# Another order for the pieces between the steps of the first down projection, and a later request for one weight block

## The chip, the core and the metric

The kernel runs on one core of a Trainium2 chip. The time is device microseconds (us) of one execution, smaller is better. The core's engines each work through an instruction queue of their own, in order: TensorE (PE; the profile counts its weight loads apart, as PEld), VectorE (DVE), ScalarE (ACT), GpSimd (POOL) and SyncE (SP). Here SP and POOL mostly issue DMA transfers. Engines wait for each other by semaphores.

## The reference

A transformer block over 2048 tokens of width 576, in bfloat16: a modulated layer norm, local attention with 32 heads of 18 (each token sees itself and seven earlier ones, two apart), an output projection, and a gated feed-forward of width 4608, with six modulation rows computed from a condition vector. Cut to what matters:

```python
mod = (_silu(c) @ w_mod).reshape(1, 6, 1, -1)            # sa, ca, ga, sb, cb, gb
h = _layernorm(x) * (1 + ca) + sa
q, k, v = split_heads(h @ wqkv)                          # 32 heads of 18
logits = einsum('bhsd,bhswd->bhsw', q, k[:, :, s - 2 * w]) * 18 ** -0.5   # w = 0..7, masked where s < 2w
o = einsum('bhsw,bhswd->bhsd', softmax(logits), v[:, :, s - 2 * w])
x = x + ga * (o @ wo)
h = _layernorm(x) * (1 + cb) + sb
x = x + gb * (((h @ w_gate) * (h @ w_up)) @ w_down)
```

## The kernel before, in words

**Tokens.** The 2048 tokens are 16 tiles of 128. Attention goes by chunks of 256 tokens (two tiles; chunks 0 to 7). The feed-forward goes by five groups of tiles, `GROUPS = [(0, 2), (2, 6), (6, 10), (10, 13), (13, 16)]`: chunk 0 alone, then chunks 1 and 2, then 3 and 4, and so on. The width 576 is four rows of 128 and one of 64; 4608 is 36 tiles f in nine weight blocks of four.

**Stages.** For each group, `gate_up` (from L847) goes through the 36 f: 18 matmuls, each on one half of PE's rows, fill two PSUM banks (`pg`, `pu`); ACT copies them out (L874, L875) and DVE multiplies them into `hh` (L880). After every fourth f, `ahead` (L892) asks for the next block of gate and up weights, on SP's queue. Then `down_pairs` (from L906) multiplies `hh` with the down weights, whose blocks POOL's queue loads (L173). For the first group, the down stage is 32 steps of 0.49 us, four to a block, each of four 512-wide and four 64-wide half matmuls (`acc` and `accr`, all issued in the helper `half`, L558), and then the last block in four runs. Four of the eight PSUM banks hold these sums; the other four make two pairs, which the pieces below take in turn. A third piece waits until the first one's pair has been read out.

**Pieces.** All work of later chunks is cut into pieces that are put between the steps. After step n, the pieces of the list at n are issued, in order; `dbg[0]` (L1466) is the plan of the first down stage, a list of (n, pieces) in which a pair of pieces takes n and n + 1. Since every engine's queue runs in order, the place in this plan is also the place in each engine's queue. The pieces, with i the chunk:

- `o_parts(i)` (L670): PE turns the attention output `o_sb` into `oT` (first and second half of the transposes); ACT copies it out (L640 ff.).
- `w1`, `w2` (`w_units`, L646): the output projection from `oT` and `wo`, in two column halves of two parts each; DVE scales it by `ga` (L656) and adds the residual `x_r` (L658): `x1`.
- `a_parts(i)` (L673): PE turns the normed input `xn` into `hT`; `mod_evict` (L630) scales and shifts it on the way out, half of it on DVE (three L327) and half on ACT (three L329).
- `q3, k3, qk4_3, v0_3, v1_3` (`qkv_units`, L685): chunk 3's query, key and value projections from `hT`.
- `av(n)` (`B_av`): the next n of chunk 2's weighted value sums on DVE (L543, L550, L552), which end in `o_sb` (L554, L555).
- `stat1`, `stat4`: statistics of chunk 1's `x1` and of chunk 4's input on ACT (L311, L314); `norms(n1)`, `norms(n4)` norm them on DVE (L322). `norm_x1_2` (L1449) does both for chunk 2's `x1`: one tile's statistics on ACT, the other's on DVE (L1456, L1457), then the norms (L322, L1462).
- `b_parts(i)` (L679): as `a_parts`, from the normed `x1` to `h2T`, which the next `gate_up` reads; `t2_2` is `b_parts(2)`. Normed tiles `ln_xn` have two buffers.

`a_parts(4)` and the projections of chunks 4 and 5 lie in the second `gate_up`, the latter between the f that `units` (L1478) names.

**Loads.** `gb_row` (L1367) runs right before the first step. It issues, on POOL and SP, down blocks 1 to 4, chunk 2's value rows (`b_ld(2, 0)`, `b_ld(2, 1)`: `vsh`, 1152 KB each) and the second group's gate/up blocks 10 and 11, and `behind` makes the latter wait until down block 3 has landed. Block 9, the first that the second `gate_up` uses, has been asked for in `ahead(0, 6)`, in the last third of the first `gate_up`. Down blocks 5, 6, 8 and 7 follow (in this order) as steps free their buffers; block 7 is used from step 28.

Of the kernel before, what the change touches and what calls it, by code (L numbers as in the profile page):

```python
# [21 lines left out]
KT = 5  # L22
# [6 lines left out]
FT = FF // P  # L29
# [6 lines left out]
FB = 4  # L36
# [12 lines left out]
def kernel(  # L49
# [97 lines left out]
    NBLK = FT // FB  # L147
# [224 lines left out]
    aa, bb, h2T, x1 = {}, {}, {}, {}  # L372
# [257 lines left out]
    def mod_evict(dst, cols, vi, kf=KF, on_dve=True):  # L630
        n = P * len(cols)

        def out_(a, b):
            for m in range(KF):
                modulate(dst(m), (a, b)[m // 2][:, m % 2, 0:n], m, vi + 1, vi, on_dve and m < 2)
            for h, t in enumerate((a, b)):
                modulate(half_of(dst(KF), h), t[:, 2, 0:n // 2].rearrange("p (c t) -> p c t", t=64), kf, vi + 1, vi, on_dve and h == 0)
        return out_
# [31 lines left out]
    def o_parts(i):  # L670
        return parts(lambda: turn_unit(o_sbs[i % 2], (0, 1), o_evict))

    def a_parts(i):  # L673
        def make():
            a_tiles(i)
            return turn_unit(aa[i]["xn"], (0, 1), mod_evict(lambda m: aa[i]["hT"][:, m, :], (0, 1), 0, KT))
        return parts(make)

    def b_parts(i, cols=(0, 1)):  # L679
# [212 lines left out]
    def ahead(gi, n):  # L892
        g = gi * NBLK + n + 2
        if gi > 0:
            load_wgu(g)
        elif n in (1, 2, 3):
            load_wgu(g + 2)
        elif n == 4:
            load_wgu(NBLK - 1)
        elif n == 5:  # L900
            load_pair_rows()
            load_wo_rows()
        elif n == 6:
            load_wgu(NBLK)

    def down_pairs(gi, hh, bg):  # L906
        for piece in bg.get(-1, ()):
            piece()
        t0, t1 = GROUPS[gi]
        nj = t1 - t0  # L910
        steps = down_steps(nj)
        acc = [ps([P, 512], F32, "acc") for _ in range(2)]
        accr = [ps([P, 2, 64], F32, "accr") for _ in range(3 if nj == 3 else 2)]
        acc += [ps([P, 512], F32, "acc") for _ in range(nj - 2)]
        o_ts, t_r = {}, {}
        seen, written, order, synced = set(), {}, [0], [-1]
        left = {("a", j): 2 * FT for j in range(nj)} | {("r", j): 2 * FT for j in range(nj)}

        def mm(kind, j, r, f):
            bank = (kind, j) if kind == "a" else (kind, j % len(accr))  # L920
            dst = acc[j][:] if kind == "a" else accr[j % len(accr)][:, j // len(accr), :]
            cs = slice(0, 512) if kind == "a" else slice(512, D)
            last_r, n, m = written.get(bank, (r, -1, None))
            if last_r != r and n > synced[0]:
                swap_after(m)
                synced[0] = n
            rows = (LO, HI)[r]
            left[kind, j] -= 1
            m = half(dst, hh[rows, f, js(j)], wd_blk[gi * NBLK + f // FB][rows, f % FB, cs], bank not in seen, left[kind, j] == 0)
            seen.add(bank)  # L930
            written[bank] = (r, order[0], m)
            order[0] += 1

        def pair(kind, lo, hi):
            for r, (j, f) in enumerate((lo, hi)):
                mm(kind, j, r, f)

        def gate(j):
            o_ts[j] = gup.tile([P, 512], BF, name="o_t", tag="g_sb" if j % 2 else "u_sb")
            nc.vector.tensor_tensor(o_ts[j][:], acc[j][:], gb_bc[:, 0:512], ALU.mult)  # L940

        def gate_r():
            t = smp.tile([P, nj, 64], BF, name="t_r", tag="tree")
            for k, a in enumerate(accr):
                n = len(range(k, nj, len(accr)))
                nc.vector.tensor_tensor(t[:, k:nj:len(accr), :], a[:, 0:n, :],
                                        gb_bc[:, None, 512:D].to_broadcast([P, n, 64]), ALU.mult)
            t_r[0] = t

        for n, (lo, hi, r_early, loaded) in enumerate(steps):  # L950
            fs = list(zip(lo, hi))
            for k, (a, b) in enumerate(fs):
                if r_early and k == len(fs) - 1:
                    pair("r", a, b)
                    pair("a", a, b)
                else:
                    pair("a", a, b)
                    pair("r", a, b)
            if loaded is not None and (gi > 0 or loaded not in (4, 5)):
                load_wd((5, 6, NBLK - 1, 7)[loaded] if gi == 0 and loaded < 4 else gi * NBLK + loaded + 3)  # L960
            for piece in bg.get(n, ()):
                piece()
        f0 = FT - FB

        def run(kind, a, b):
            for f in range(f0, FT):
                pair(kind, (a, f), (b, f))

        if nj == 2:
            run("r", 0, 1)  # L970
            run("a", 0, 1)
            for piece in bg.get(len(steps), ()):
                piece()
            run("r", 1, 0)
            gate_r()
            run("a", 1, 0)
            gate(0)
            gate(1)
        elif nj == 4:
            run("r", 0, 1)  # L980
            run("r", 2, 3)
            run("a", 0, 1)
            run("a", 2, 3)
            run("r", 1, 0)
            run("r", 3, 2)
            gate_r()
            run("a", 1, 0)
            gate(0)
            gate(1)
            run("a", 3, 2)  # L990
            gate(2)
            gate(3)
        else:
            for k, (lo, hi) in enumerate(cycle_of_three(f0)):
                for a, b in zip(lo, hi):
                    pair("a", a, b)
                    pair("r", a, b)
                if k == 4:
                    gate(1)
            gate_r()  # L1000
            gate(0)
            gate(2)
        assert not any(left.values())
        for j in range(nj):
            xt = x1[(t0 + j) // ST][(t0 + j) % ST]
            r0 = (t0 + j) * P
            nc.vector.tensor_tensor(xt[:, 0:512], o_ts[j][:], xt[:, 0:512], ALU.add)
            nc.vector.tensor_tensor(xt[:, 512:D], t_r[0][:, j, :], xt[:, 512:D], ALU.add)
            nc.sync.dma_start(out_flat[r0:r0 + P, :], xt[:])
        load_wd(gi * NBLK + NBLK + 2)  # L1010
# [362 lines left out]
    def gb_row():  # L1373
        p_t = mod_row(lambda k: wm5[:, k, :] if k < KF else wm5r[:], sc32)
        rows = gup.tile([P, RN], BF, name="gb_rows", tag="u_sb")
        nc.scalar.copy(rows[0:32 * RG, :], p_t[0:32 * RG, :])
        nc.sync.dma_start(gd[:], rows[0:32 * RG, :])
        nc.sync.dma_start(gb_bc[:], bass.AP(gd.tensor, gd.offset, [[0, P], [32 * RN, RG], [1, RN]]))
        behind(load_wd(1), wgu_in[7])
        load_wd(2)  # L1380
        b_ld(2, 0)
        place_pair_rows()
        wd3 = load_wd(3)
        for g in (1, 2):
            behind(load_wgu(NBLK + g), wd3)
        b_ld(2, 1)
        load_wd(4)


    def av(n):  # L1390
        for p in av2[:n]:
            p()
        del av2[:n]
# [20 lines left out]
    w1, w2, w3, w4, w5, w6, w7 = [w_parts(i) for i in range(1, NCH)]  # L1414
# [17 lines left out]
    def norms(n):  # L1432
        for j in range(ST):
            n["norm"](j)
# [14 lines left out]
    def norm_x1_2():  # L1449
# [11 lines left out]
        for d0, s0, n in ((0, 0, D), (D, D - 64, 64)):  # L1461
# [2 lines left out]
    q3, k3, qk4_3, v0_3, v1_3 = qkv_units(3, [(0, 0, 5)])[0]  # L1464
    t2_2 = b_parts(2)
    dbg = {0: at((-1, [gb_row]), (-1, lambda: n3["rsq"]()), (0, o_parts(1)), (0, lambda: (norms(n3), load_x(5))), (2, lambda: av(4)),  # L1466
                 (5, a_parts(3)), (6, stat4), (6, lambda: av(2)), (7, w1[0]), (9, w1[1]), (10, stat1), (11, q3), (12, lambda: av(3)), (13, k3), (14, lambda: av(14)),
                 (15, qk4_3), (17, v0_3), (19, lambda: norms(n1)), (20, o_parts(2)), (22, lambda: (norms(n4), load_x(6))), (22, b_parts(1)), (24, w2[0]),
                 (25, w2[1]), (26, norm_x1_2), (28, v1_3), (FT - FB - 1, t2_2)),
           1: at((0, o_parts(3)), (3, w3[0]), (6, w3[1]), (8, lambda: b_ln(3)), (9, o_parts(4)), (10, lambda: b_norm(3)), (13, b_parts(3)),  # L1470
                 (13, lambda: a_ln(6)), (16, w4[0]), (18, lambda: (a_norm(6), load_x(8))), (19, w4[1]), (21, lambda: b_ln(4)),
                 (23, a_parts(6)), (24, lambda: b_norm(4)), (28, b_parts(4))),
# [2 lines left out]
                 (24, a_parts(7)), (25, lambda: b_norm(6)), (29, b_parts(6, (0,)))),  # L1475
           3: at(*apart(3, b_parts(6, (1,))), *apart(9, o_parts(7)), *apart(16, w7[0]), *apart(23, w7[1]), (27, lambda: b_ln(7)),
                 (33, lambda: b_norm(7)), *apart(41, b_parts(7)))}
    units = {1: qkv_units(4, [(2, 0, 1), (3, 1, 2), (4, 2, 3), (5, 3, 4), (6, 4, 5)]) | qkv_units(5, [(29, 0, 1), (30, 1, 2), (31, 2, 3), (32, 3, 4), (33, 4, 5)]),  # L1478
             2: qkv_units(6, [(0, 0, 1), (1, 1, 2), (2, 2, 3), (3, 3, 4), (4, 4, 5)]),
             3: qkv_units(7, [(0, 0, 3), (1, 3, 4), (2, 4, 5)])}  # L1480
    for gi in range(NG):
# [37 lines left out]
```

## Time and profile before

| | |
|---|---|
| runs | 546.92, 545.93, 546.80 us; median 546.8 |
| the profiled execution | 546.86 us, of which the span is 545.2 |
| PE busy | 535.3 us, 98% of the span |
| DVE, ACT, POOL busy | 319.8, 268.5, 72.0 us |
| granted TensorE clock | 1.000 |
| first gate/up ends, down stage begins | 88 us |
| second gate/up begins | 121 us |
| DMA in this stretch (88 to 116 us) | 305 to 336 GB/s |

The span is the time from the first to the last instruction that the profile shows. A line of the waits names the engine and the line that waited, what released it, the time in all, how often and the longest. A row of the timeline gives start, duration, engine, line, operation, output and inputs, and in brackets the engine's idle time before it with the releaser; "issue" means that the profile shows nothing that it waited for. A matmul's duration is longer than its step to the next, since matmuls overlap.

### The profile page before, as it was taken

The page shows a single profiled execution, that of the slowest core. Times are in us where ns is not written, and L with a number is a line of the kernel's source. Part 1 is how long each engine was busy: PE and PEld are TensorE (multiplying, and loading weights), DVE is VectorE, ACT ScalarE, POOL GpSimd, SP SyncE. Part 2 cuts the span into 40 slices and gives each one's busy share as a digit, 9 for nine tenths or more (in the row PEclk, how much of TensorE's full clock was granted, in tenths as well). Part 3 has the DMA queues.
Part 4 walks back from the last instruction along what each step waited for, and adds up shares of the span by engine and source line. Part 5 has one row for each costly group of instructions (what it writes and reads, how often), then busy time and mean ns, then how long its engine had stood idle before and what let it go on. Part 6 is the DMA issues. An engine that isn't in the chain of part 4 may idle for free.

```text
span 545.2 us, 17482 instructions
## 1 busy us (share of the span) xinstructions
PE 535.3 (98%) x7579; PEld 339.6 (62%) x7579; DVE 319.8 (59%) x775; ACT 268.5 (49%) x657; POOL 72.0 (13%) x117
## 2 busy tenths in 40 slices
PE   7999999999999999999999999999999999999997
PEld 4788887656544698755544445556665555666564
DVE  7887898966469862557357795454537624322203
ACT  2766687755655763213656653224566511556500
POOL 4301224130001001112000101111100023100010
PEclk9999999999999999999999999999999999999999
DMA  8999999968336844346533774444785766965021
GB/s 261 279 266 316 352 303 340 338 196 293 96 115 217 275 136 143 112 117 231 210 108 127 259 235 156 133 132 133 237 269 155 231 198 176 348 193 175 1 88 34
DMA packets 70775, 108.83 MB, mean 200 GB/s; under 512 B 4234, under 2 KB 58458, under 8 KB 70698
## 3 DMA queue, kind: packets, MB, share of 16 engines
q1 hardware_dynamic: 59440, 61.76, 37.2%
q0 software_dynamic: 11168, 45.81, 25.5%
q8 instruction: 59, 0.97, 0.8%
q14 instruction: 18, 0.15, 0.1%
q10 hardware_dynamic: 90, 0.15, 0.1%
HBM read 103.22 MB, written 4.48 MB: 198 GB/s over the span
## 4 chain that ended last, share of the span: by engine, by line
PE 85%; DMA 8%; DVE 3%; ACT 2%; issue 1%; SPq 0%; POOL 0%; POOLq 0%; ACTq 0%; DVEq 0%
PE pg L558 26%; PE pu L558 21%; PE acc L558 17%; PE pp L558 9%; PE acc L1050 4%; DMA vsh<-vd 3%; DMA wgu<-in_B_w_up_dram 2%; PE accr L558 2%; DMA wv<-in_A_wqkv_dram 1%; PE lg L486 1%; DMA wmA<-in_w_mod_dram 1%; DVE prod L476 1%; PE pq L415 1%; PE po L759 1%; PE tr_pA L605 1%
## 5 line engine op out<-in xcount | busy, mean ns | idle before, releaser
L558 PE MATMUL pg<-h2T,wgu 64*128 64x512 bf16 (+2 forms) x1440 | 280.4, 333 | 1.0 <-issue 1.0
L558 PE MATMUL pu<-h2T,wgu 64*128 64x512 bf16 (+2 forms) x1440 | 278.7, 333 | 0.0
L558 PEld LDWEIGHTS <-wgu 64*128 64x128 bf16 x2880 | 148.4, 94 | 97.7 <-issue 1.3
L874 ACT CAST u_sb<-pu 128x512 bf16<-128x512 f32 (+2 forms) x180 | 90.1, 501 | 126.2 <-PE pg L558 118.2
L880 DVE TENSOR_TENSOR hh<-g_sb,u_sb 128x512 bf16<-128x512 bf16 (+2 forms) x180 | 66.3, 370 | 104.8 <-ACT g_sb L875 102.6
L558 PE MATMUL acc<-wd,hh 64*128 64x512 bf16 x888 | 118.3, 377 | 0.0
L558 PEld LDWEIGHTS <-hh 64*128 64x128 bf16 x1872 | 66.9, 94 | 43.9 <-issue 0.2
L875 ACT CAST g_sb<-pg 128x512 bf16<-128x512 f32 (+2 forms) x180 | 91.5, 508 | 0.0
L558 PE MATMUL accr<-wd,hh 64*128 64x64 bf16 x888 | 80.2, 189 | 0.0
L558 PE MATMUL pg<-h2T,wgr 64*128 64x512 bf16 (+2 forms) x180 | 60.1, 334 | 0.5 <-ACT h2T L329 0.5
L558 PE MATMUL pu<-h2T,wgr 64*128 64x512 bf16 (+2 forms) x180 | 60.1, 334 | 0.0
L173 POOL DMA_DIRECT2D wd<-in_B_w_down_dram x38 | 28.7, 755 | 176.6 <-PE accr L558 74.3
L476 DVE TENSOR_TENSOR prod<-qT,kT 128x1280 bf16<-128x1280 bf16 x54 | 42.9, 820 | 6.7 <-ACT kT L393 6.7
L543 DVE TENSOR_TENSOR vsh<-vsh,attn 128x1152 bf16<-128x1152 bf16 x56 | 40.4, 751 | 0.7 <-DMA vsh<-vd 0.7
L656 DVE TENSOR_TENSOR x<-pp,ga_bc 128x288 bf16<-128x288 f32 x28 | 12.0, 452 | 36.9 <-PE pp L558 36.9
L558 PEld LDWEIGHTS <-wgr 64*128 64x128 bf16 x360 | 18.6, 94 | 14.0 <-issue 2.1
L558 PE MATMUL pp<-hT,wqk 64*128 64x256 bf16 x360 | 22.6, 269 | 0.4 <-ACT hT L329 0.4
L329 ACT ACTIVATE h2T<-tr_pB,modc 128x256 bf16<-128x256 bf16 (+2 forms) x26 | 11.4, 507 | 21.2 <-PE tr_pA L605 20.5
L558 PEld LDWEIGHTS <-wqk 64*128 64x128 bf16 x360 | 18.5, 94 | 3.9 <-issue 0.7
L555 POOL COPY o_sb<-o_sb 128x64 bf16<-128x64 bf16 x10 | 3.0, 303 | 135.4 <-DVE o_sb L554 135.4
L550 DVE TENSOR_TENSOR vsh<-vsh 128x1152 bf16<-128x1152 bf16 x28 | 20.5, 750 | 0.0
L558 PE MATMUL pp<-wo,oT 64*128 64x288 bf16 x252 | 20.2, 283 | 0.2 <-DVE hT L327 0.2
(265 smaller groups left out, 591.9 us busy)
## 6 DMA issues: line engine op xcount, KB each, us to landing
wgu<-in_B_w_gate_dram SPq DMA_DIRECT2D x45, 512.0 KB, 4.2
wgu<-in_B_w_up_dram SPq DMA_DIRECT2D x45, 512.0 KB, 5.8
wd<-in_B_w_down_dram POOLq DMA_DIRECT2D x38, 576.0 KB, 4.4
vsh<-vd POOLq DMA_DIRECT2D x14, 1152.0 KB, 8.9
x_r<-in_A_x_dram SPq DMA_DIRECT2D x8, 288.0 KB, 7.7
vsh<-in_B_w_down_dram POOLq DMA_DIRECT2D x4, 576.0 KB, 8.3
out_dram<-x SPq DMA_DIRECT2D x15, 144.0 KB, 7.6
x_t<-in_A_x_dram SPq DMA_DIRECT2D x7, 288.0 KB, 7.0
```

Source lines behind the costliest of these rows:

```text
L173: return nc.gpsimd.dma_start(wb[:], B_w_down[r0:r0 + FB * P, :].rearrange("(k p) n -> p k n", p=P))
L329: nc.scalar.activation(dst, s, ACTF.Identity, bias=modc[:, vi_shift, m:m + 1], scale=modc[:, vi_scale, m:m + 1])
L415: nc.tensor.matmul(pq[:, gi, :], lhsT=qk_w(kt, m), rhs=hT[:, kt, :], start=(kt == 0), stop=(kt == KT - 1))
L476: nc.vector.tensor_tensor(prod[:], aa[i]["qT"][:], aa[i]["kT"][:, :, off:off + CH], ALU.mult)
L543: nc.vector.tensor_tensor(v, v, at, ALU.mult)
L550: nc.vector.tensor_tensor(vsh[:, d], vsh[:, d], vsh[:, 4 + 2 * s:6 + 2 * s], ALU.add)
L558: return nc.tensor.matmul(dst, lhsT=lhs, rhs=rhs, start=first, stop=last, skip_group_check=True)
L656: nc.vector.tensor_tensor(x1[i][j][:, cs], t[:, 0, :], ga_bc[:, cs], ALU.mult)
L874: nc.scalar.copy(u[:, 0:N], pu[:, 0:N])
L875: nc.scalar.copy(g[:, 0:N], pg[:, 0:N])
L880: nc.vector.tensor_tensor(hh[:, f, 0:N], g[:, 0:N], u[:, 0:N], ALU.mult)
L1050: nc.tensor.matmul(a[:], lhsT=hh[:, f, js(j)], rhs=wb[:, f % FB, cs], start=(f == 0), stop=(f == FT - 1))
```

## The change

- `a_parts(4)` is evicted by ACT alone: `mod_evict` gets `on_dve = (i != 4)`.
- Gate/up block 9 is asked for in `gb_row`, ahead of 10 and 11 and like these behind down block 3; `ahead(0, 6)` asks for nothing.
- The plan `dbg[0]` has another order: w1 to qk4_3 come one step later; v0_3's second part moves from 18 to 21, behind `o_parts(2)`, which comes one step earlier (19, 20); w2 comes two steps earlier (22 to 24), `norm_x1_2` too (24), and `b_parts(1)` moves from 22, ahead of w2, to 25, behind `norm_x1_2`; v1_3 comes one step earlier; `t2_2` moves from 31 and the middle of the last block to 30 and 31, so that the place inside the last block's runs is no longer needed.
- In the second `gate_up`, chunk 4's q comes after f = 3 instead of 2, and its k and fourth q/k tile both after f = 4.

```diff
-            return turn_unit(aa[i]["xn"], (0, 1), mod_evict(lambda m: aa[i]["hT"][:, m, :], (0, 1), 0, KT))
+            return turn_unit(aa[i]["xn"], (0, 1), mod_evict(lambda m: aa[i]["hT"][:, m, :], (0, 1), 0, KT, i != 4))
...
-        elif n == 6:
-            load_wgu(NBLK)
...
             run("r", 0, 1)
             run("a", 0, 1)
-            for piece in bg.get(len(steps), ()):
-                piece()
             run("r", 1, 0)
...
         wd3 = load_wd(3)
-        for g in (1, 2):
+        for g in range(3):
             behind(load_wgu(NBLK + g), wd3)
...
-                 (5, a_parts(3)), (6, stat4), (6, lambda: av(2)), (7, w1[0]), (9, w1[1]), (10, stat1), (11, q3), (12, lambda: av(3)), (13, k3), (14, lambda: av(14)),
-                 (15, qk4_3), (17, v0_3), (19, lambda: norms(n1)), (20, o_parts(2)), (22, lambda: (norms(n4), load_x(6))), (22, b_parts(1)), (24, w2[0]),
-                 (25, w2[1]), (26, norm_x1_2), (28, v1_3), (FT - FB - 1, t2_2)),
+                 (5, a_parts(3)), (6, stat4), (6, lambda: av(2)), (8, w1[0]), (10, w1[1]), (11, stat1), (12, q3), (13, lambda: av(3)), (14, k3), (15, lambda: av(14)),
+                 (16, qk4_3), (18, v0_3[:1]), (18, lambda: norms(n1)), (19, o_parts(2)), (20, lambda: (norms(n4), load_x(6))), (21, v0_3[1:]), (22, w2[0]), (23, w2[1]),
+                 (24, norm_x1_2), (25, b_parts(1)), (27, v1_3), (FT - FB - 2, t2_2)),
...
-    units = {1: qkv_units(4, [(2, 0, 1), (3, 1, 2), (4, 2, 3), (5, 3, 4), (6, 4, 5)]) | qkv_units(5, [(29, 0, 1), (30, 1, 2), (31, 2, 3), (32, 3, 4), (33, 4, 5)]),
+    units = {1: qkv_units(4, [(3, 0, 1), (4, 1, 3), (5, 3, 4), (6, 4, 5)]) | qkv_units(5, [(29, 0, 1), (30, 1, 2), (31, 2, 3), (32, 3, 4), (33, 4, 5)]),
```

## The prediction, made before the changed kernel had run

> **What bounds the kernel.** I read the page first, for the engine that sets the time; then the waits from 79 to 135 us, for what stops it around the change; then the timeline at each stop; then the transfers in windows.
>
> ```profile
> span 545.2 us, 17482 instructions
> PE 535.3 (98%) x7579; PEld 339.6 (62%) x7579; DVE 319.8 (59%) x775; ACT 268.5 (49%) x657; POOL 72.0 (13%) x117
> PE 85%; DMA 8%; DVE 3%; ACT 2%; issue 1%; SPq 0%; POOL 0%; POOLq 0%; ACTq 0%; DVEq 0%
> ```
>
> TensorE is busy 98% of the span and is 85% of the chain that ended last. The change takes no matmul away and adds none, so only PE's idle time can move: six stops between 79 and 135 us, which the waits name.
>
> ```profile
> PE pg L558 <- issue: 1.0, 1, 1.0
> PE pg L558 <- ACT h2T L329: 0.5, 1, 0.5
> PE pp L558 <- ACT hT L329: 0.4, 1, 0.4
> PE tr_pB L605 <- DVE rs L533: 0.3, 1, 0.3
> PE tr_pA L605 <- DVE ln_xn L322: 0.3, 1, 0.3
> PE pp L558 <- DVE hT L327: 0.2, 1, 0.2
> ```
>
> The timeline places five of them, in order of time (the sixth, at t2, stands with its part below); the bracket is PE's idle time and its releaser:
>
> ```profile
> 82.18 0.27 PE L558 MATMUL pg<-h2T,wgu 64*128 64x256 bf16 x1 [0.95 <-issue]
> 89.12 0.20 PE L605 MATMUL tr_pB<-ident,o_sb 64*128 64x64 bf16 x1 [0.35 <-DVE rs L533]
> 95.72 0.79 PE L558 MATMUL pp<-wo,oT 64*128 64x288 bf16 x10 [0.18 <-DVE hT L327]
> 121.15 0.37 PE L558 MATMUL pg<-h2T,wgr 64*128 64x512 bf16 x1 [0.47 <-ACT h2T L329]
> 126.94 1.27 PE L558 MATMUL pp<-hT,wqk 64*128 64x256 bf16 x20 [0.35 <-ACT hT L329]
> ```
>
> An idle bracket is shorter than the time lost, since a matmul row overlaps the next. I measure a stop as the start-to-start step less that of undisturbed neighbours: 1.1, 0.5, 0.34, 0.64 and 0.51 us. The windows tell of the transfers (busy PE, PEld, DVE, ACT, POOL; clock; DMA share; GB/s):
>
> ```profile
> 75.00:82.00 7.00, 6.23 (x115) 6.03 (x111) 6.93 (x17) 6.53 (x22) 3.59 (x4) 1.00 1.11 268
> 82.00:92.00 10.00, 9.48 (x189) 7.55 (x190) 8.10 (x27) 7.36 (x25) 4.40 (x5) 1.00 0.99 334
> 92.00:104.00 12.00, 11.82 (x222) 8.38 (x220) 11.86 (x23) 10.12 (x27) 1.69 (x3) 1.00 1.00 336
> 104.00:116.00 12.00, 12.00 (x236) 7.76 (x232) 8.29 (x23) 6.25 (x19) 1.50 (x2) 1.00 0.93 305
> 116.00:121.00 5.00, 4.24 (x74) 2.11 (x71) 3.11 (x13) 3.30 (x11) 2.88 (x5) 1.00 0.36 80
> ```
>
> The DMA engines are full from 75 to 116 us, the clock is 1.00, and DVE is as full as PE from 92 to 104. The profiled execution took 546.86 us: span 545.2 and 1.66 around it. It lies 0.06 over the median of the three runs (546.8). The change is under the measurement's bound if it is below 0.2%, 1.09 us.
>
> **The change part by part.** Steps of the down stage are 0.49 us each; the last w2 matmuls have left PE at 113.61 in the trace, and I count from that point, called E.
>
> *w1 one step later* (95.72): hT's three L327 ended at 95.66; 0.49 us more lets them end before. Gain 0.34.
>
> *t2 behind norm_x1_2* (117.16). Step 31 ends at 117.16, and the last block's first matmul starts at 118.44: 1.28 us, of which the transposes need 0.18. The rest, 1.10, waits for the two norms:
>
> ```profile
> 117.64 0.20 PE L605 MATMUL tr_pA<-ident,ln_xn 64*128 64x64 bf16 x1 [0.32 <-DVE ln_xn L322]
> 117.71 0.64 DVE L1462 TENSOR_SCALAR ln_xn<-x,ln_mvb 128x576 bf16<-128x576 bf16 x2
> 119.73 1.37 ACT L329 ACTIVATE h2T<-tr_pB,modc 128x256 bf16<-128x256 bf16 x3 [1.61 <-PE tr_pA L605]
> 119.77 0.98 DVE L327 TENSOR_SCALAR h2T<-tr_pA,modc 128x256 bf16<-128x256 bf16 x3 [1.43 <-PE tr_pA L605]
> ```
>
> The changed order puts two more steps and b_parts(1) between, so this wait as such goes: gain 1.10. But t2 takes the pair of PSUM banks that b_parts(1) used (four banks are free, and v1_3 has the other pair), and b_parts(1) is now evicted behind norm_x1_2 on DVE and on ACT. What is late next: DVE's L1462 ended at 118.35, E + 4.74; three L327 of 0.98 bring E + 5.72; the first L311 also has to wait for b_parts(1) to leave its xn buffer (two exist), up to 0.2: E + 5.9. PE arrives at six steps (2.94), b_parts(1) (0.30) and v1_3 (0.61 + 0.49): E + 4.34. So a new stop of 1.4 to 1.6; I take 1.5. Were the buffer wait nothing it would be 1.4; were DVE and ACT each to start 0.5 late, as behind the 0.46 of an L656, 2.0; below 1.4 the order of DVE's queue excludes.
>
> *t2's second half before the last block* (121.15). It runs a step and a block, 2.0 + 0.49 us, before gate/up, and its eviction on ACT takes 1.37: h2T is ready some 0.4 before PE needs it. Gain 0.64; if t2 slips by more than 0.4 past the 1.5, it returns one for one.
>
> *Chunk 4's q one f later, evicted on ACT alone* (126.94). ACT's three L329 took 1.39 (from 125.50), six take 2.78 and end at 128.28; PE comes to q at 126.3 + 2.2 (an f) = 128.5. Gain 0.51, with 0.2 to spare; a bound of 0.3 the other way if ACT's u_sb and g_sb (0.6 each) come between; I take a loss of 0.05. DVE gets 0.98 back that nobody waits for.
>
> *Pieces that move to tighter places.* o_parts(2) comes one step and half a v0_3 (0.5) earlier. Its o_sb is ready when DVE's L555 ends, at 106.33; PE would arrive at about 106.4. w2[0] first needs oT 1.62 us after the last transposes and has 1.5 of cover. From 0 to 0.6 lost (DVE is full there; norms(n1) and norms(n4), L322, stand behind the value sums as before); I take 0.15, as the one measured margin is short by 0.1. q3, k3, qk4_3 keep 0.2 to 0.4 of margin each, and cost nothing unless PE gains more than that on ACT.
>
> *Block 9's load to behind wd3.* SP no longer issues its two halves (75.16, 75.59; landed 85.17 and 91.26) but after 93.8, with two more issues ahead of x_t (103.04, 5.90 for two), which moves some 4 us; it is needed tens of us later. Block 9 would land near 108, as the first of SP's three did (108.61), and is needed at 120.5; the last near 117. 1 MB less in the full stretch from 75 on is 3.1 us of 336 GB/s. It can shorten the two stops named "issue" (82.18; 89.12, where PEld says issue too): between them PE and PEld issue exactly 256 instructions, and the page counts 59 packets of queue "q8 instruction", one per 256 of PE's 2 x 7579 instructions: they are waits for instructions. The next two crossings, at 95.5 and 103.1 in equally full windows, show no such stop, so a stop is no certainty. Worth 0 (the queue is full of other things) to 1.6 (both go). I take 0.5: the later stop, which has 13 us of lighter transfers before it; the earlier has 6.
>
> The Trainium skill ("Runtime: NRT & Kernel Launch", section "Instruction fetch mechanics") says that PE refills 16 KiB blocks of 256 instructions ahead of use and that crossing one is "mostly hidden". The 256 agrees with the trace; the 0.95 idle at 82.18 does not look hidden. By the page alone this term is 0 and the sum 545.97.
>
> **Sum:** 0.34 + 1.10 + 0.64 + 0.51 + 0.5 - 1.5 - 0.05 - 0.15 = 1.39 gained: 546.86 - 1.39 = 545.47, say 545.5.
>
> **Rivals.**
> *Both instruction stops go*: 1.1 more, 544.4. For it: the first is 7 us behind the removed load. Against: SP's and POOL's other transfers keep the 75 to 82 window full.
> *No instruction stop goes, or PE's gain is eaten by DVE*: if PE comes 0.5 earlier to o_parts(2), o_sb is the wait (L555 at 106.33 moves only if the value sums start earlier, and they waited 0.75 at 92.01 for vsh). Either leaves 0.4 to 0.9 of gain: 546.0 to 546.5.
> *Other side: three gate/up blocks in a row on SP make wd7 late.* POOL issued it at 104.17 and it landed at 112.18, 8.0 us on; step 28 used it at 114.10. In the new order both come 0.84 earlier by the first and the fetch term, and the use 0.61 later by v1_3's first half: issue at about 103.3, use at 113.9: a flight over 10.6 stops PE, over 13.1 (1.39 + 1.09 late) the kernel is slower by more than 0.2%. At the 14.3 us that the median up block took in this stretch the wait is 3.7 and the time 549.2; at up 9's 15.7, 550.6. Against: SP's queue was busy with gate/up until 113.21 before, too, and wd7 took 8.0.
>
> The Trainium skill ("DMA: Bandwidth & Descriptors", section "Queues, rings and completion order") has each DMA engine take turns between queue rows packet by packet, which would share bandwidth with SP's row but not put wd7 behind its megabytes; the 8.0 us beside a busy SP queue agrees.
>
> **The numbers.** The forecast (545.0 to 545.9) has 0.42, of which 0.07 lies within 0.2% (above 545.71); both stops 0.13; nothing from the stops 0.30, all within 0.2%; the other side 0.15, of which 0.13 is beyond 547.9 and 0.02, with a wd7 that is only a little late, within 0.2%. Faster 0.48, same 0.39, slower 0.13. The range 544.3 to 547.4 takes in the first three cases and the lightest of the fourth.
>
> **What the profile after would show.** No idle at w1's matmuls, at the first matmul of the second gate/up and at chunk 4's q; one new stop of about 1.5 at t2's first transposes, released by L327 or L329 of h2T (shorter: the bank wait is mis-sized; released by ln_xn: the norms are); the "issue" stops at 82 and 89 shorter or as they were; wd7's landing before step 28. I am wrong if o_parts(2) or q3 show stops of over 0.5, or if an instruction stop appears at another multiple of 256.

## The result and the profile after

Over 22 runs of each, the changed kernel takes 545.13 us and the kernel before 546.36 (medians): 0.9981 of it, 95% interval 0.9973 to 0.9989. The profiled execution took 545.02, its span is 543.3. The forecast was 545.5, faster.

The page of the changed kernel, and the waits of TensorE from 79 to 135 us (in total, times, longest):

```profile
span 543.3 us, 17484 instructions
PE 535.3 (99%) x7579; PEld 338.1 (62%) x7579; DVE 318.6 (59%) x772; ACT 269.4 (50%) x660; POOL 71.4 (13%) x117
```

```profile
PE tr_pA L605 <- ACT h2T L329: 0.8, 1, 0.8
PE pg L558 <- issue: 0.4, 1, 0.4
PE tr_pB L605 <- DVE h2T L327: 0.2, 1, 0.2
```

PE's busy time is the same 535.3. The waits for `hT` (L327 and L329), for `h2T` ahead of gate/up and for the norms are gone; there is one new stop, whose two lines name `h2T` again, but with the transposes of t2 as what waits. In the timeline of the changed kernel (L1458 is what was L1462):

```profile
112.54 0.68 ACT L311 ACTIVATE ln_xn<-x 128x576 bf16<-128x576 bf16 x1 [4.26 <-PE tr_pA L605]
...
115.11 1.35 ACT L329 ACTIVATE h2T<-tr_pB,modc 128x256 bf16<-128x256 bf16 x3
...
115.37 0.64 DVE L1458 TENSOR_SCALAR ln_xn<-x,ln_mvb 128x576 bf16<-128x576 bf16 x2
...
115.92 0.97 DVE L327 TENSOR_SCALAR h2T<-tr_pA,modc 128x256 bf16<-128x256 bf16 x3
...
116.51 0.19 PE L605 MATMUL tr_pA<-ident,ln_xn 64*128 64x64 bf16 x1 [0.78 <-ACT h2T L329]
...
116.95 0.20 PE L605 MATMUL tr_pB<-ident,ln_xn 64*128 64x64 bf16 x1 [0.25 <-DVE h2T L327]
...
119.81 0.38 PE L558 MATMUL pg<-h2T,wgr 64*128 64x512 bf16 x1
```

When the norms begin, `b_parts(1)` is still to be read out: L327 stands behind L1458 in DVE's queue, ends at 116.89, and PE goes on at 116.95. The second gate/up starts at 119.81 with no idle time before it. The windows of the transfers (busy PE, PEld, DVE, ACT, POOL; clock; DMA share; GB/s):

```profile
75.00:82.00 7.00, 6.58 (x124) 5.75 (x120) 6.93 (x17) 6.33 (x21) 3.24 (x4) 1.00 1.09 282
82.00:92.00 10.00, 9.93 (x209) 7.55 (x205) 8.87 (x29) 7.20 (x25) 4.12 (x5) 1.00 0.68 226
92.00:104.00 12.00, 12.00 (x220) 8.52 (x214) 11.68 (x24) 10.61 (x28) 2.24 (x3) 1.00 0.99 341
104.00:116.00 12.00, 11.62 (x216) 7.28 (x211) 8.08 (x25) 6.43 (x21) 0.75 (x1) 1.00 1.05 344
```

The load is gone from 82 to 92 us (0.68 instead of 0.99), and made up for from 104 to 116. From 75 to 82 the share has hardly moved.

**Where the time went.** Since no matmul is added or taken away, the trace can be cut at the same matmul in every kernel. I cut it at four: the first of the first gate/up, the last 512-wide one of step 7 (93.05 before), the first of the second gate/up, and the first of its seventh f (140.00 before). The table has all the profiles of this study, in us:

```
kernel                              setup   A: to     B: to     C: to      D: to
                                            step 7    gate/up   7th f      the end
before                              47.62   45.44     28.10     18.84      405.15
before, once more (e11)             47.35   44.63     28.34     18.85      405.16
before, 48 matmuls more (e7)        48.31   44.76     27.96     18.85      405.14
before + load later (e2)            47.26   44.62     28.10     18.85      405.14
before + q later, ACT alone (e8)    46.78   44.62     28.09     18.32      405.15
before + q later (e9)               49.83   44.63     28.20     18.32      405.16
after, plan of before (e3)          47.36   44.60     28.02     18.32      405.17
after                               47.20   44.69     27.93     18.30      405.17
after, once more (e10)              48.08   45.03     27.93     18.30      405.16
after, q at f = 2 (e4)              47.09   44.64     27.93     20.11      405.15
after, load as before (e1)          47.12   44.64     28.16     18.30      405.15
after, t2 late (e6)                 48.25   44.63     27.56     18.30      405.15
after, b_parts(1) early (e5b)       46.78   44.96     27.32     18.30      405.16
after, both (e5)                    47.05   45.14     26.96     18.30      405.17
```

Columns C and D repeat within 0.03 us, B is 27.96 to 28.34 with the code of before, and 27.93 twice with the one after. The setup and A do not repeat: 46.8 to 49.8, and 44.6 to 45.4 with the same code. Of the 1.9 us between the first two spans, 0.42 is setup and 0.75 is A, which the same code also shows; only the rest, 0.71, is the change at work: 0.17 in B and 0.54 in C. That is 0.13% of the time, a ratio of 0.9987.

### The profile page after: what moved, and what is told of

Same layout as the page of the kernel before. It is cut to its first block, busy times and chain, and to the rows that moved or that the text cites. A ratio compares the mean times of both kernels' runs of the same rounds, so it can differ in the third digit from the quotient of the medians.

```text
span 543.3 us, 17484 instructions
## 1 busy us (share of the span) xinstructions
PE 535.3 (99%) x7579; PEld 338.1 (62%) x7579; DVE 318.6 (59%) x772; ACT 269.4 (50%) x660; POOL 71.4 (13%) x117
## 4 chain that ended last, share of the span: by engine, by line
PE 88%; DVE 6%; DMA 2%; ACT 1%; issue 1%; SPq 0%; ACTq 0%
PE pg L558 26%; PE pu L558 21%; PE acc L558 18%; PE pp L558 9%; PE acc L1046 4%; PE accr L558 2%; PE lg L486 1%; DMA wv<-in_A_wqkv_dram 1%; DVE prod L476 1%; DVE vsh L543 1%; DMA wmA<-in_w_mod_dram 1%; PE pq L415 1%; PE po L759 1%; PE tr_pA L605 1%; DVE hh L880 1%
## 5 line engine op out<-in xcount | busy, mean ns | idle before, releaser
L329 ACT ACTIVATE h2T<-tr_pB,modc 128x256 bf16<-128x256 bf16 (+2 forms) x26 | 11.4, 506 | 20.5 <-PE tr_pA L605 19.7
L555 POOL COPY o_sb<-o_sb 128x64 bf16<-128x64 bf16 x10 | 3.0, 303 | 135.5 <-DVE o_sb L554 135.5
```

What stands on the lines that cost most here:

```text
L329: nc.scalar.activation(dst, s, ACTF.Identity, bias=modc[:, vi_shift, m:m + 1], scale=modc[:, vi_scale, m:m + 1])
```

## The experiments

Times are medians, beside runs of the kernel before on the same chip. The ratios are those on record with each run, with their 95% intervals; they are to the kernel before, but not the quotients of the medians. Three groups ran: e1, e3, e4, e5 (before: 545.96), then e2, e7, e8, e5b (545.73), then e10, e6, e9, e11 (546.16).

**e1: the load as before.**

```diff
+        elif n == 6:
+            load_wgu(NBLK)
...
-        for g in range(3):
+        for g in (1, 2):
```

> The changed kernel, with block 9 asked for where it was before. Theory (the stops named issue are waits for instructions that the transfers delay): the steps at 81.21 and 87.88 grow again from 0.69 and 0.26 to about 1.2 and 0.5, and the time to 545.13 + 0.82 = 545.9. Rival (their length varies from execution to execution, whatever the transfers): no difference, 545.1.

Measured 545.38, 0.9990 (0.9978 to 1.0001). Neither step came back: with the old load there was no stop at 81 us at all, and A is 44.64. So the old place of the load is not enough to make these stops. B is 0.23 longer than in the changed kernel, at one place. DVE's waits name it:

```profile
DVE vsh L543 <- DMA vsh<-vd: 0.3, 1, 0.3
```

In the profile before it is longer:

```profile
92.01 2.76 DVE L543 TENSOR_TENSOR vsh<-vsh,attn 128x1152 bf16<-128x1152 bf16 x4 [0.75 <-DMA vsh<-vd]
```

There chunk 2's value rows landed at 91.91; in the changed kernel they landed at 88.70, and DVE does not wait for them. In e1 it waits 0.27; DVE then comes 0.44 later to `hT`'s L327 (93.76 against 93.31), and w1's second half loses 0.23. So the load can cost B something, by way of DVE, but not always: of the six profiles with the load in its old place only these two have the wait (in e11 the rows landed at 88.61), and of the eight with the new place none.

**e2: nothing but the load.**

```diff
-        elif n == 6:
-            load_wgu(NBLK)
...
-        for g in (1, 2):
+        for g in range(3):
```

> The kernel before, with nothing but block 9's load behind down block 3. If the load sets the stops for instructions, they go or shrink and the time falls by 0.8. If they vary by the execution (the run with the load put back showed none at all at that place), the time is that of before within 0.3, and the profile may show stops of any length there.

Measured 545.99, 0.9998 (0.9980 to 1.0017); B, C and D as before. By itself the load brings nothing that these runs can tell; in the old plan w1's second half still came right behind L327.

**e7: the same program, 96 instructions further on.**

```diff
-        for _ in range(n):
-            nc.tensor.matmul(idle[:], lhsT=zero[:, 0:P], rhs=zero[:], start=True, stop=True, skip_group_check=True)
+        for _ in range(n):
+            for c in range(4):
+                nc.tensor.matmul(idle[:, js(c)], lhsT=zero[:, 0:P], rhs=zero[:, js(c)], start=True, stop=True, skip_group_check=True)
```

> The kernel before, with each of the 16 idle 512-wide matmuls of the setup as four of 128: 48 matmuls and 48 weight loads more, all before 6 us. If the stops named issue come at the 256th instruction, wherever that falls, they are 96 instructions earlier in the program: at the 30th of the first gate/up's 36 f instead of the 32nd, near 79.5, and near 86.3; the one at 95.72, if it is L327's, stays where it is (if it is a wait for instructions too, it goes to 93). If they belong to what the program does there, all stay. Time as before within 0.3.

Measured 546.69, 1.0003 (0.9982 to 1.0023). The stop at w1 stayed with its matmul (95.61): it is L327's. This had to be tested, since in the kernel before a count of 256 instructions ends at that very matmul (95.72, not 95.5 as the prediction has it). The earlier stop named "issue" did not come, at 79.0 or elsewhere. The later one did, small, at 86.22 where 86.3 had been forecast, and no other profile stops at that matmul (lines of e7 from 207 on are one later; PEld from 86 to 86.5 us):

```profile
86.22 0.33 PEld L559 LDWEIGHTS <-wgu 64*128 64x128 bf16 x7 [0.20 <-issue]
```

So the place of the later stop moved with the count of instructions, as forecast; whether PE stops at such a place, and for how long, differs between executions.

**e10 and e11: both kernels once more.** No edit.

> The changed kernel itself, beside the next two on one chip. From the second part of the down stage on the profile repeats within 0.05; the step at 81.21 (0.69 in the first profile) may be anything from 0.1 to 1.5 if it varies by the execution, and is 0.5 to 0.9 if the load's new place has set it.

> The kernel before, once more, for its profile. If the stops named issue are a property of the execution, the 1.22 and 0.54 of the first profile need not be there; all the others (95.72, 117.16, 121.15, 126.94) are, at the same lengths within 0.05.

e10: 545.69, 0.9996 (0.9987 to 1.0004), and a stop of 1.10 where the first profile had 0.69, outside the 0.5 to 0.9 expected if the load's new place set it. e11: 546.03 (one run), and no stop there. The waits of e11 are those of before without "issue" and L533, and with one more for `ln_xn` (0.15, at 90.88, ahead of chunk 3's transposes):

```profile
PE pg L558 <- ACT h2T L329: 0.5, 1, 0.5
PE tr_pA L605 <- DVE ln_xn L322: 0.5, 2, 0.3
PE pp L558 <- ACT hT L329: 0.4, 1, 0.4
PE pp L558 <- DVE hT L327: 0.2, 1, 0.2
```

*What makes the stop.* The trace records each packet of the queue "q8 instruction". I set the end of the one before the stop against the moment at which PE has issued its 2497 instructions up to there, 2489 of them weight loads and matmuls (us). e7 is not in the table, since its 2497th instruction is another one; there the packet ended at 77.45, 1.57 before PE came, and PE did not stop:

```
                 packet's end   PE is there   end to there   PE goes on after
e9                   81.48         83.15          1.67            0.01
e8                   78.55         80.11          1.56            0.00
e4                   78.92         80.41          1.49            0.11
e1                   78.96         80.44          1.48            0.03
e11 (before)         79.23         80.67          1.44            0.00
e6                   80.21         81.58          1.37            0.00
e2                   79.36         80.58          1.22            0.15
after                79.67         80.52          0.85            0.69
e3                   80.14         80.69          0.55            0.79
e10 (after)          81.14         81.40          0.26            1.10
e5b                  79.88         80.11          0.23            1.30
before               80.83         80.96          0.13            1.22
e5                   80.36         80.38          0.02            1.48
```

Where PE stops for over 0.5, the two right columns add up to 1.34 to 1.54: PE goes on about 1.45 us after the packet has ended, and hardly stops if the packet ended that much earlier. At the next crossing, 256 instructions on, four profiles have a stop of 0.20 to 0.53 (before, after, e10 and e7); it ends 1.24 to 1.65 us after its packet. So the stop is a wait for instructions, with a size that one packet's time sets.

Asking for block 9 later does not shorten it. With the load in its old place one profile of six has a stop of over 0.5 here (before; not e11, e7, e1, e8, e9), with the new place five of eight. Nor did the later load make room: in the 7 us from 27.4 us after the first gate/up's begin, the DMA share is 1.04 to 1.11 in the six and 1.08 to 1.09 in the eight. Whether the new place makes stops more frequent, and what sets the packet's time, is open. The Trainium skill ("Runtime: NRT & Kernel Launch", section "Instruction fetch mechanics") calls the cost of such a crossing "mostly hidden"; here PE hardly stopped in seven of thirteen profiles, and stopped for 0.69 to 1.48 at that place in the others.

A stop also costs less than its length. A is 44.79 on average in the six profiles and in the eight. In the profiles without the stop PE loses time behind it instead: the next f takes 1.30 to 1.35 and not 1.10, and the stretch with chunk 3's first transposes, from step 5 to step 6, takes 1.13 to 1.14 and not 0.72 to 0.88, since the norms (L322) are no earlier:

```profile
90.88 0.20 PE L605 MATMUL tr_pA<-ident,ln_xn 64*128 64x64 bf16 x1 [0.15 <-DVE ln_xn L322]
```

That row is of e11. So e3, with a stop of 0.79, has the shortest A of all (44.60), and the two stops of the first profile before, 1.1 and 0.5, make A only 0.8 longer than in e11.

**e3: the old plan.** The changed kernel with all of `dbg[0]` and the place inside the last block as before; the core of it:

```diff
+            for piece in bg.get(len(steps), ()):
+                piece()
...
-                 (16, qk4_3), (18, v0_3[:1]), (18, lambda: norms(n1)), (19, o_parts(2)), (20, lambda: (norms(n4), load_x(6))), (21, v0_3[1:]), (22, w2[0]), (23, w2[1]),
-                 (24, norm_x1_2), (25, b_parts(1)), (27, v1_3), (FT - FB - 2, t2_2)),
+                 (15, qk4_3), (17, v0_3), (19, lambda: norms(n1)), (20, o_parts(2)), (22, lambda: (norms(n4), load_x(6))), (22, b_parts(1)), (24, w2[0]),
+                 (25, w2[1]), (26, norm_x1_2), (28, v1_3), (FT - FB - 1, t2_2)),
```

> The changed kernel, with the plan of the first down stage as it was before, t2's second half inside the last block. By the profile after (the stage itself lost 0.54 against before and the stop at its end, 0.64, went): 0.1 more than the changed kernel, 545.2. By the prediction's own terms (0.34 + 1.10 + 0.64 - 1.5 - 0.15 = 0.43): 545.6. If the plan's order carries the whole gain, 546.4.

Measured 545.12, 0.9990 (0.9981 to 0.9999). B is 28.02 against 27.93, C and D the same: in this pair the new plan is worth 0.09 us. Against all seven profiles with the old plan (27.96 to 28.34) it is worth 0.18 on average, not 0.43. Nearly all that it removes, the new stop takes back.

**e4, e8, e9: chunk 4's q.** e4 is the changed kernel with the old `units`, `a_parts(4)` still on ACT alone; e8 is the kernel before with the changed kernel's `units` and its `a_parts(4)`; e9 the kernel before with the new `units` only.

```diff
-    units = {1: qkv_units(4, [(3, 0, 1), (4, 1, 3), (5, 3, 4), (6, 4, 5)]) | ...
+    units = {1: qkv_units(4, [(2, 0, 1), (3, 1, 2), (4, 2, 3), (5, 3, 4), (6, 4, 5)]) | ...
```

> The changed kernel, with chunk 4's q, k and fourth tile after f = 2, 3 and 4 again, and a_parts(4) still on ACT alone. Theory: q stops for hT, now for six L329 instead of three, so the stop is 0.5 + 1.4 less the 0.1 that ACT has free: up to 1.9, 547.0; if only the 0.5 returns, 545.7. Rival (q waits for nothing that the later f gives): 545.1.

> The kernel before, with nothing but a_parts(4) on ACT alone and chunk 4's q one f later. By the prediction and by the profile after: the 0.51 at q goes, 545.96 - 0.5 = 545.5 against the 545.96 that the kernel before had beside the first four runs; nothing else changes. Rival: the stop only moves to k or to a later u_sb, 546.0.

> The kernel before, with nothing but chunk 4's q one f later (k and the fourth tile as in the changed kernel); a_parts(4) is still shared by DVE and ACT. If the place of q is the whole gain there, its stop goes as with ACT alone: 0.52 off the part behind the second gate/up's begin, hT being ready some 1.4 before q. If ACT alone is needed, the stop stays.

e4 measured 546.71, 1.0017 (1.0005 to 1.0029): slower than the kernel before. Its timeline has the long stop that was expected:

```profile
126.71 0.50 PE L558 MATMUL pp<-hT,wqk 64*128 64x256 bf16 x6 [1.63 <-ACT hT L329]
```

e8 measured 545.38, 0.9991 (0.9971 to 1.0010), and e9 545.59, 0.9998 (0.9986 to 1.0009); these intervals cannot tell 0.5 us from nothing, but column C can: 18.32 in both, 18.84 before, and no wait for `hT` at q. The place of q is the whole gain there. ACT alone brings nothing to PE, and makes the place necessary: without it, C is 20.11.

**e5, e5b, e6: the new stop.** In all three the changed kernel's plan is edited near its end. e5b only brings `b_parts(1)` ahead of w2; e6 only puts t2 later; e5 does both.

```diff
e5, e5b
-                 (22, w2[0]), (23, w2[1]), (24, norm_x1_2), (25, b_parts(1)), (27, v1_3)
+                 (22, b_parts(1)), (23, w2[0]), (24, w2[1]), (25, norm_x1_2), (27, v1_3)
e5, e6
-                 (FT - FB - 2, t2_2)
+                 (FT - FB - 1, t2_2)
...
             run("r", 0, 1)
+            for piece in bg.get(len(steps), ()):
+                piece()
             run("a", 0, 1)
```

> The changed kernel, with b_parts(1) ahead of w2 (22), w2 and norm_x1_2 one step later (23 to 25), t2's first half after step 31 and its second after the last block's first run. Theory (t2 waits for the banks that b_parts(1) leaves late): no L327 or L329 releases t2 any more; it waits for norm_x1_2, at E + 4.74 against 4.04 for PE, 0.7 in place of 1.6: 544.2. Rival (the norms end late by themselves, and the bank wait only covers them): the wait stays 1.5, 545.1. If t2's eviction no longer ends before gate/up, its first matmul shows a stop, and the gain is less by that.

> The changed kernel, with b_parts(1) ahead of w2 as in the run before, but t2 at steps 30 and 31 as in the changed kernel. If the banks made t2's stop of 1.6: what remains is the wait for the norms, E + 4.74 (the buffer wait of L311 goes) against PE's 5 steps and v1_3 at E + 3.55: 1.2, released by ln_xn; 0.4 to 0.5 faster than the changed kernel. If t2's place made it, the time is that of the changed kernel or above, and the gain of the run before came from step 31 and the run behind it.

> The changed kernel, with only t2 moved: first half after step 31, second after the last block's first run; b_parts(1) stays behind norm_x1_2. If the banks hold t2 until E + 5.96, PE comes 0.49 later and waits 0.49 less, the eviction of 1.4 still fits before the 1.9 of the remaining runs, and the kernel is 0.4 to 0.5 faster than the changed one. If the time came from t2's distance to gate/up, it is no faster.

e5b: 544.52, 0.9970 (0.9949 to 0.9991); e6: 544.86, 0.9984 (0.9976 to 0.9993); e5: 544.29, 0.9965 (0.9952 to 0.9977). Column B falls from 27.93 by 0.61, 0.37 and 0.97: together as much as the two apart. Of e5b's 0.61, 0.51 lies between the begin of step 30 and that of step 31, where t2's first transposes are (2.04 to 1.53). In e5b's waits of TensorE and its weight loads, from 86 to 130 us, no L327 and no L329 is left:

```profile
PEld L605 <- DVE ln_xn L322: 0.4, 1, 0.4
PEld L558 <- PE acc L558: 0.4, 1, 0.4
PEld L605 <- DVE ln_xn L1458: 0.2, 1, 0.2
PEld L366 <- issue: 0.2, 1, 0.2
PEld L558 <- issue: 0.2, 1, 0.2
```

In e6 the stop is still the banks', and shorter, since PE comes later to it:

```profile
PE tr_pA L605 <- ACT h2T L329: 0.3, 1, 0.3
PE tr_pB L605 <- DVE h2T L327: 0.3, 1, 0.3
PE tr_pA L605 <- DVE ln_xn L322: 0.2, 1, 0.2
```

So the banks of `b_parts(1)` made the new stop, as forecast. e5 (six runs) is the fastest kernel of the study: 0.35% under the kernel before, and 0.97 us under the changed one by column B.

## Why the prediction was right, and where not

It gave faster by 1.39; the runs gave 1.23 by the medians of 22, and the trace 0.71 that is the change's own. The second series (0.9996) shows how little of such a difference a dozen runs can hold; both intervals contain 0.9987 to 0.9989, which is what 0.71 us makes. Term by term:

- *w1 one step later, 0.34*: the stop is gone. The step alone is not always enough: in e1, with the load back and the value rows late, 0.23 of the stop is there. The prediction priced the two apart.
- *t2 behind the norms, 1.10, and the banks, 1.5*: the right mechanism. The w2 matmuls left PE at 110.93 (E); L327 ended at E + 5.96, forecast E + 5.9; PE went on at 116.95, 1.68 after E + 4.34, the time at which PE was to come. The term was 0.18 too small, in three like parts: 1.56 was taken as 1.5, L327 ended 0.06 later (the first L311 waited 0.34 for its buffer, from E + 1.27 to E + 1.61, and not 0.2), and PE went on 0.06 after it.
- *h2T ahead of gate/up, 0.64*: gone, no idle time at 119.81.
- *q of chunk 4, 0.51*: column C, 0.54. The loss of 0.05 set against it did not come.
- *o_parts(2) and oT, 0.15*: o_parts(2) waited for nothing (L555 ended at 105.19, the transposes began at 105.28); w2's first half lost 0.20 to oT.
- *The stops for instructions, 0.5*: this is the step that failed. That they are waits for instructions holds; that block 9's later load shortens them does not, and the traffic ahead of the earlier one did not even fall. Both numbers that the term was made from, 1.1 and 0.5, came from one execution, and the next one of the same kernel (e11) had neither. Nor is a stop's length its price: both together cost 0.8, not 1.6. The term measured 0.00, the difference of A's averages over fourteen profiles; that the first two profiles differ by 0.75 in A is the luck of two executions. Without the term the sum was 0.89, against 0.71 measured, and the forecast would have been 546.0, within 0.2%.

In B alone the forecast was 0.43 (0.34 + 1.10 + 0.64 - 1.5 - 0.15) and the first two profiles give 0.17; the two stops that were mis-sized, 0.18 and 0.05, are 0.23 of the 0.26 between them. So the forecast's direction was right by its terms, but that its size came so near to the medians is partly luck: half a microsecond of it rests on the term that failed, and where the medians get more than 0.71 from stays open.

Of the rivals, the late wd7 did not come: issued at 101.78, it landed at 109.72, 7.9 us on, with all six gate/up transfers on SP's queue; 8.0 before. That both stops for instructions go is what e1, e4 and e2 show, but not because of the change. "Nothing from the stops" describes best what the change did, though its 546.0 to 546.5, counted from a run of 546.86, lies above the median.

## What to carry to other kernels

When a plan moves a piece past another, ask which PSUM banks it now inherits, and from whom: the stop that a new order removes can come back as the wait for a bank that is read out late, because its eviction stands behind other work in an in-order queue. Here the plan removed stops of 2.1 us and got about 0.2; moving `b_parts(1)` out of the way afterwards gave 0.6 more, and t2 later as well 1.0. Price a stop by what waits behind it, not by its length: one of 0.79 cost nothing here. And cut two traces at the same instructions before explaining the difference of their spans: of 1.9 us, 1.2 belonged to the execution and not to the kernel.

## What was not expected of the hardware

- A wait for instructions of 0 to 1.48 us at the same matmul of the same code, set by when one 16 KB packet ends: PE went on 1.34 to 1.54 us after it in the six profiles with a stop of over 0.5. In e7, with 96 instructions more ahead of it, the next such stop came at 86.22, where the count put it.
- The time until the first gate/up, with the same code, was 46.8 to 49.8 us.
